# Attention weights turned by DMA: six of eight transposes leave TensorE, and tokens are dealt to the logits' column groups in another way

## The chip, the cores and the metric

The kernel runs on one core of a Trainium2 chip. The metric is the device time of one execution in microseconds, here the median of the runs shown. A profiled execution also gives the span of its trace, which is a little shorter than its device time.

## What is computed

One transformer block with adaptive layernorm over 2048 tokens of width 512, all in bf16. Attention has 32 heads of 16 and looks only at eight earlier tokens, two apart; the second half is a gated feed-forward of width 1792.

```python
def _A_ref(x, wqkv, wo):
    B, S, D = x.shape
    H = 32
    Dh = D // H
    W, dil = (8, 2)
    qkv = (lambda x, *d: x.transpose(*d))((x @ wqkv).reshape(B, S, 3, H, Dh), 2, 0, 3, 1, 4)
    ...
    off = jnp.arange(W) * dil
    idx = pos[:, None] - off[None, :]
    mask = idx >= 0
    ...
    logits = jnp.einsum('bhsd,bhswd->bhsw', q, kg) * scale
    logits = jnp.where(mask[None, None, :, :], logits, -1000000000.0)
    attn = _softmax(logits, axis=-1)
    o = jnp.einsum('bhsw,bhswd->bhsd', attn, vg)
    return (lambda x, *d: x.transpose(*d))(o, 0, 2, 1, 3).reshape(B, S, D) @ wo
...
sa, ca, ga, sb, cb, gb = ...            # six vectors of silu(c) @ w_mod
h = _layernorm(x, axis=-1) * (1 + ca) + sa
x = x + ga * _A_ref(h, A_wqkv, A_wo)
h = _layernorm(x, axis=-1) * (1 + cb) + sb
x = x + gb * _B_ref(h, B_w1, B_w3, B_w2)   # (silu(h @ w1) * (h @ w3)) @ w2
```

## The kernel before

The 2048 tokens are 16 tiles of 128. A tile goes through these steps; the lines are those of the profile.

- Statistics of x on VectorE (L555, L556), a reciprocal square root on GpSimd, and the normalised tile on VectorE (L576). It is transposed on TensorE (L636) or by DMA, and ScalarE or VectorE applies scale and shift (L644, L621). In groups of 2, 2, 4, 4 and 4 tiles, q and k come out transposed (L691), v with tokens on partitions (L711); v is stored to a scratch in DRAM.
- Logits, tile by tile: VectorE multiplies q with eight shifted views of k at once (L742, the first product, 4096 elements a partition), and 16 matmuls with a 0/1 matrix sum over the 16 elements of each head (L752). These use TensorE as four groups of 32 columns, and each group q takes 32 tokens of the tile; the logits stand with 32 heads of group q on partitions 32q to 32q+31, and shift and token in the free dimension. For tile 0, one more matmul first adds the mask of shifts that reach before token 0 (L749).
- Softmax for a pair of tiles at once: four VectorE instructions on PSUM (L764, L769, L794, L796 and the last, L797, which writes the weights to SBUF) with ScalarE's exponential in between (L782). A pair is named here by its first tile: pair 4 is tiles 4 and 5.
- The weights must then stand with token and shift on partitions and heads in the free dimension. For each pair, TensorE transposes four blocks into PSUM (L807) and ScalarE copies them to SBUF (L811).
- Values: per tile four DMA loads of v from the scratch bring shift and token onto partitions ("value loads", sb_vsh and sb_vshx), VectorE multiplies them with the weights (L827), and TensorE sums over the shifts in eight matmuls (L855, "the sums"). ScalarE copies the result (L861), a DMA transpose on SP's queue turns it (sb_ot, "the outputs"), four matmuls apply wo (L867), and VectorE adds the residual (L871).
- Feed-forward in groups of 2, 2, 4, 4, 2 and 2 tiles: layernorm with sums from ScalarE (L590, L601) and GpSimd, transposition, then 14 units of two times four matmuls (L883), silu on ScalarE (L889), gate product on VectorE (L892); then the second matmuls (L921, L909), the output add (L931) and a store.

The six vectors of the modulation are columns computed by matmuls with one column each: L504 for the first layernorm, L531 twice for the two gates, L487 for the second layernorm. wo and w2 are scaled by the gates on VectorE (L946, L952).

Nothing of the order is left to a scheduler at run time: ORDER lists all operations in one sequence, and each engine executes its own in that sequence; nearly all DMAs are issued by SP, in order. An operation waits on semaphores for what it reads and for the last users of the buffer it overwrites; SLOTS says which buffer of a pool each value gets (eight PSUM banks, three for v, three for softmax, and so on). So an instruction that waits holds up all that stand behind it on its engine, and a DMA that waits holds up SP's queue.

Of the kernel before, what the change touches and what calls it, by code (L numbers as in the profile page):

```python
# [6 lines left out]
ACT = mybir.ActivationFunctionType  # L7
# [3 lines left out]
P = 128  # L11
S = 2048
D = 512
H = 32
DH = 16
W = 8
# [57 lines left out]
class Program:  # L74
# [41 lines left out]
    def dma(self, out, in_, key, packets, r=(), w=(), part=(), after=(), eng="sp", cost=450, group=None, transpose=False,  # L116
            store=False, again=False, lat=None):
        nc = self.nc

        def fn(e):  # L120
            a = out() if callable(out) else out
            b = in_() if callable(in_) else in_
            with nc.allow_non_contiguous_dma(reason="layout"):
                return e.dma_start(a, b, transpose=True) if transpose else e.dma_start(a, b)  # L124

        n, size = packets
        each = -(-n // 16)
        ns = 600 if transpose else each * (126 if again else packet_ns(size))
        o = self.op(eng, fn, cost, key, r=r, w=w, part=part, after=after, dma=(each, ns, *(lat if lat else (900, 200) if store else (900, 500) if transpose else (1300, 600))))
        if group is not None:  # L130
            group.append(o)
            o.group = group
        return o
# [135 lines left out]
AC_OLD = ()  # L269
LN1 = [[0, 1], [2, 3], [4, 5, 6, 7], [8, 9, 10, 11], [12, 13, 14, 15]]  # L270


def _build(p, A_x, A_wqkv, A_wo, B_w1, B_w3, B_w2, c, w_mod, out):
# [23 lines left out]
    atb = [sb([P, 2, 32, W], bf, f"attn{i}") for i in range(NSM)]  # L297
    alb = [sb([P, 2, 8, H], bf, f"al{i}") for i in range(3)]
# [94 lines left out]
    for y in range(2):  # L393
# [3 lines left out]
                                           pattern=[[-DIL, W], [1, 2], [2, 16]], channel_multiplier=0), 400, k, w=[vbefore])  # L397
# [333 lines left out]
    def logits(Ts):  # L731

        vl = Val("ps_l", psum)
        for i, T in enumerate(Ts):
# [11 lines left out]
            def red(e, i=i, T=T, vp=vp):  # L746
                c0 = vl.at * 512 + i * W * 32
                if T == 0:
                    e.matmul(PALL[0:32, c0:c0 + W * 32], ones[:, 0:32], before[:], start=True, stop=False, tile_position=(0, 0))  # L749
                for ft in range(KT):  # L750
                    for q in range(4):
                        ins = e.matmul(PALL[32 * q:32 * q + 32, c0:c0 + W * 32], E_sb[:, ft, :], bass.AP(vp.at, ft * P + 32 * q, [[W * KT * P, P], [KT * P, W], [1, 2], [2, 16]]),  # L752
                                       start=(ft == 0 and (T > 0 or q > 0)), stop=(ft == KT - 1), tile_position=(0, 32 * q))
# [35 lines left out]
    def softmax(Ts, vl, ve, vx_):  # L789
# [7 lines left out]
        p.op("dve", lambda e: e.tensor_tensor(ve.at[0][:, 0:n], bass.AP(PALL, bank(vl).offset, [[8 * 512, P], [W * 32, n], [1, 32], [32, W]]),  # L797
                                              bass.AP(ve.at[2], 0, [[64, P], [32, n], [1, 32], [0, W]]), ALU.mult),
             74 + 267 * n, k, r=[vr, vx_], w=[va], hold=[ve, vl], lead=o, lock=False)
        vt, val = Val("ps_at", psum), Val("al", alpool)  # L800

        def turn(e):
            b = bank(vt).bitcast(bf)
            for i in range(n):
                at = b[:, i * 256:(i + 1) * 256].rearrange("p (q y h) -> p q y h", q=4, y=2)
                for y in range(2):
                    ins = e.transpose(at[:, :, y, :], bass.AP(ve.at[0], i * W * 32 + y * 16 * W, [[2 * W * 32, P], [1, P]]), ident[:])  # L807
# [3 lines left out]
        p.op("act", lambda e: e.activation(val.at[:, 0:n].rearrange("p n g h -> p (n g h)"), bank(vt).bitcast(bf)[:, 0:2 * n * P], ACT.Copy),  # L811
# [264 lines left out]
```

## Time and profile before

| | before |
|---|---|
| median of the runs shown | 243.6 us |
| fastest run shown | 243.37 us |
| profiled execution, its own time | 242.82 us |
| span of its trace | 241.1 us |
| granted TensorE clock | 1.0 |
| TensorE (PE) busy | 230.4 us, 1781 matmuls |
| VectorE (DVE) busy | 179.6 us |
| ScalarE (ACT) busy | 138.7 us |
| GpSimd (POOL) busy | 30.9 us |
| moved by DMA | 38.85 MB, 46317 packets |

In the profile a row of a group names line, engine and operation, tile written and tiles read, shapes and count, then the busy time and the mean duration of one, then the idle time ahead of them and what ended it. Matmuls overlap in the pipeline, so the duration of one (219 ns for a 128x128 transpose) is longer than what one adds to the engine's time; the chain and the timeline show the latter, as the time that a run of so many took. "SPq" is the issue of a DMA, whose data land later.

### The profile page before, as it was taken

Reading aid. Unit: us, or ns where it says so; the run is one execution under the profiler, and the core shown is the slowest. Engines: PE = TensorE matmul, PEld = TensorE weight load, DVE = VectorE, ACT = ScalarE, POOL = GpSimd, SP = SyncE. Lnnn points to the kernel's source line nnn. Section 1 sums busy time; section 2 is a strip of 40 time slices with the busy share of each in tenths; the row PEclk is TensorE's granted clock in tenths of the full one; section 3 lists DMA queues with packets and bytes.
Section 4 is the critical chain, followed back from the end, with each engine's and each line's share of the span. In section 5 each row is a group of like instructions: output and inputs, shape, how many; then the busy total and the mean of one; then the engine's idle time right before and its main releaser. Section 6 shows DMA issues by size and latency. Waiting matters only on the chain.

```text
span 241.1 us, 4538 instructions
## 1 busy us (share of the span) xinstructions
PE 230.4 (96%) x1781; PEld 136.8 (57%) x1806; DVE 179.6 (75%) x279; ACT 138.7 (58%) x267; POOL 30.9 (13%) x66
## 2 busy tenths in 40 slices
PE   7988999979999999999799999999999999999995
PEld 4856454544587685564345444444565584485874
DVE  5697999979989999898999999764565044423542
ACT  2296497688999744955964578646537253140300
POOL 4332060004001000250005301001001000000000
PEclk9999999999999999999999999999999999999999
DMA  6999999999979996693893882253220300000103
GB/s 222 370 327 327 163 262 234 287 282 343 331 134 253 283 270 115 160 272 99 213 256 119 195 197 46 66 141 98 76 79 0 46 0 0 3 22 0 48 0 109
DMA packets 46317, 38.85 MB, mean 161 GB/s; under 512 B 21704, under 2 KB 37080, under 8 KB 46296
## 3 DMA queue, kind: packets, MB, share of 16 engines
q1 hardware_dynamic: 46288, 38.56, 62.5%
q8 instruction: 14, 0.23, 0.4%
q14 instruction: 7, 0.06, 0.1%
q10 hardware_dynamic: 8, 0.00, 0.0%
HBM read 29.62 MB, written 4.21 MB: 140 GB/s over the span
## 4 chain that ended last, share of the span: by engine, by line
PE 50%; ACT 1%; DMA 1%; issue 1%; DVE 0%; SPq 0%
PE pall L883 30%; PE pall L921 12%; PE pall L867 3%; PE pall L909 3%; DMA sb_h<-sb_xn 1%; ACT sb_h L621 1%; PE pall L855 1%; PE pall L752 1%; PE pall L807 0%; ACT sb_al L811 0%; DVE sb_o L931 0%; SPq L124 0%
## 5 line engine op out<-in xcount | busy, mean ns | idle before, releaser
L883 PE MATMUL pall<-sb_h,sb_w 128*128 128x256 bf16 (+1 forms) x665 | 101.8, 307 | 1.0 <-ACT sb_h L621 0.6
L883 PEld LDWEIGHTS pall<-sb_h,sb_w 128*128 128x128 bf16 x672 | 64.8, 98 | 36.2 <-issue 1.5
L892 DVE TENSOR_TENSOR sb_hh<-sb_sg,pall 128x256 bf16<-128x256 bf16 (+1 forms) x84 | 40.4, 505 | 32.1 <-PE pall L883 32.0
L889 ACT ACTIVATE sb_sg<-pall 128x256 bf16<-128x256 f32 (+1 forms) x84 | 36.2, 455 | 43.4 <-PE pall L883 37.3
L921 PE MATMUL pall<-sb_w,sb_hh 128*128 128x512 bf16 x189 | 43.7, 379 | 0.4
L742 DVE TENSOR_TENSOR sb_pq<-sb_q,sb_kT 128x4096 bf16<-128x4096 bf16 x16 | 36.3, 2282 | 0.0
L921 PEld LDWEIGHTS pall<-sb_w,sb_hh 128*128 128x128 bf16 x196 | 19.1, 98 | 21.0
L691 PE MATMUL pall<-sb_h,sb_wqkv 128*128 128x512 bf16 (+1 forms) x159 | 30.3, 336 | 0.1
L827 DVE TENSOR_TENSOR sb_vsh<-sb_vsh,sb_al 128x4096 bf16<-128x4096 bf16 x12 | 27.3, 2286 | 2.4 <-ACT sb_al L811 2.2
L621 ACT ACTIVATE sb_h<-sb_h,sb_modc 128x512 bf16<-128x512 bf16 (+1 forms) x24 | 16.3, 733 | 13.0 <-DMA sb_h<-sb_xn 13.0
L691 PEld LDWEIGHTS pall<-sb_h,sb_wqkv 128*128 128x128 bf16 x160 | 15.1, 98 | 12.2 <-ACT sb_h L644 0.5
L931 DVE TENSOR_TENSOR sb_o<-pall,sb_x 128x512 bf16<-128x512 f32 (+1 forms) x18 | 10.9, 627 | 11.8 <-PE pall L921 8.7
L586 POOL TENSOR_SCALAR sb_nm<-sb_sx 128x2 f32<-128x2 f32 x8 | 3.7, 465 | 115.9 <-DVE sb_x L871 115.9
L590 ACT ACTIVATE sb_xn<-sb_x,sb_nm 128x512 bf16<-128x512 bf16 x16 | 11.4, 714 | 11.7 <-POOL sb_nm L586 11.7
L867 PE MATMUL pall<-sb_wo,sb_ot 128*128 128x512 bf16 x60 | 15.0, 379 | 1.1 <-DMA sb_ot<-sb_ac 0.5
L711 PE MATMUL pall<-sb_wqkv,sb_h 128*128 128x512 bf16 x58 | 15.0, 379 | 0.3 <-issue 0.2
L644 ACT ACTIVATE sb_h<-pall,sb_modc 128x256 bf16<-128x256 bf16 (+1 forms) x18 | 9.9, 616 | 8.6 <-DVE sb_modc L509 6.7
L601 ACT ACTIVATE sb_xn<-sb_x,sb_nb,sb_rs 128x512 bf16<-128x512 bf16 x16 | 12.6, 806 | 3.7 <-POOL sb_nb L599 3.7
L871 DVE SCALAR_TENSOR_TENSOR sb_x<-pall,sb_x 128x512 bf16<-128x512 f32 x16 | 11.0, 688 | 2.3 <-PE pall L867 2.3
L701 ACT ACTIVATE sb_kT<-pall 128x512 bf16<-128x512 f32 x16 | 9.6, 606 | 4.7 <-PE pall L691 4.7
L555 DVE BATCH_NORM_STATS2 sb_st<-sb_x 128x6 f32<-128x512 bf16 x16 | 10.4, 678 | 1.3 <-DMA sb_x<-in_A_x_dram 1.3
L721 ACT ACTIVATE sb_v<-pall 128x512 bf16<-128x512 f32 x16 | 9.6, 612 | 2.4 <-DMA v_scratch_dram<-sb_v 2.3
(87 smaller groups left out, 208.6 us busy)
## 6 DMA issues: line engine op xcount, KB each, us to landing
sb_vsh<-v_scratch_dram SPq DMA_DIRECT2D x48, 256.0 KB, 4.6
sb_vshx<-v_scratch_dram SPq DMA_DIRECT2D x16, 256.0 KB, 4.3
sb_w<-in_B_w_dram SPq DMA_DIRECT2D x6, 512.0 KB, 5.6
sb_w<-in_B_w_dram SPq DMA_DIRECT2D x6, 384.0 KB, 6.0
v_scratch_dram<-sb_v SPq DMA_DIRECT2D x16, 128.0 KB, 5.9
out_dram<-sb_o SPq DMA_DIRECT2D x14, 128.0 KB, 1.9
sb_wqkv<-in_A_wqkv_dram SPq DMA_DIRECT2D x6, 256.0 KB, 6.0
sb_x<-in_A_x_dram SPq DMA_DIRECT2D x4, 256.0 KB, 6.3
```

The lines of the kernel that those rows point to most:

```text
L590: p.op("act", lambda e, vn=vn, T=T: e.activation(vn.at[:], x_sb[:, T, :], ACT.Square, bias=nm[:, T, :], accum_out=var[:, T, :]), c_act(512 ...
L601: p.op("act", lambda e, vn=vn, T=T: e.activation(vn.at[:], x_sb[:, T, :], ACT.Identity, bias=nb[:, T, :], scale=rs[:, NT + T, :]), c_act(5 ...
L621: return e.activation(vh.at[:, ft, 0:n * P], vh.at[:, ft, 0:n * P], ACT.Identity, bias=modc[:, 8 * which + ft:8 * which + ft + 1], scale=m ...
L691: ins = e.matmul(bank(vp)[:, j * n:(j + 1) * n], wqkv[:, t, col:col + P], vh.at[:, t, 0:n], start=(t == ORDER[0] and j == 0), stop=(t == O ...
L711: ins = e.matmul(bank(vp), vh.at[:, t, tt * P:(tt + 1) * P], wqkv[:, t, 2 * D:3 * D], start=(t == ORDER[0]), stop=(t == ORDER[-1]))
L742: return e.tensor_tensor(vp.at[:], in0, in1, ALU.mult)
L827: return e.tensor_tensor(v_w, v_w, a_w, ALU.mult)
L867: ins = e.matmul(bank(vy), vt.at[:, ft, :], wo[:, ft, :], start=(ft == 0), stop=(ft == KT - 1))
L883: ins = e.matmul(bank(vp)[:, 0:n], wt[:, t, fi * P:(fi + 1) * P], vh.at[:, t, 0:n], start=(t == 0), stop=(t == KT - 1))
L889: p.op("act", lambda e: e.activation(vt.at[:, 0:n], bank(vgp)[:, 0:n], ACT.Silu), c_act(n), k, r=[vgp], w=[vt], table="silu")
L892: p.op("dve", lambda e: e.tensor_tensor(vh_.at[:, 0:n], vt.at[:, 0:n], bank(vup)[:, 0:n], ALU.mult), c_dve(n), k, r=[vt, vup], w=[vh_])
L921: ins = e.matmul(bank(vz), vhh[fi].at[:, tt * P:(tt + 1) * P], w2[:, fi, :], start=(fi == 0), stop=(fi == NF - 1))
```

## The change

Which 32 tokens of a tile a column group of the logits takes is changed: group q took tokens 32q to 32q+31, even ones first, then odd; now it takes 16 tokens of one parity from each half of the tile. With that, the weights of a pair are four plain blocks of 128 columns, and their transposes are what one DMA transpose of a 128x512 tile gives; the tile order on partitions after it is as before. For pairs 0 and 2 (`AT_PE`) TensorE and ScalarE still do it. For pairs 4, 6, 8, 10, 12 and 14 SP issues one DMA transpose of the shape that the outputs use. The mask for tile 0 follows the new dealing and takes two matmuls. The softmax writes the same elements in the same order; the buffers only change their shape.

ORDER and SLOTS are new as a whole: every engine's sequence changes, the early loads on SP and the places of the FFN units included. Groups, blocks, loads and gates are the same.

```diff
@@ dma(): takes hold=() and hands it on to op()
+AT_PE = (0, 2)
@@ _build
-    atb = [sb([P, 2, 32, W], bf, f"attn{i}") for i in range(NSM)]
-    alb = [sb([P, 2, 8, H], bf, f"al{i}") for i in range(3)]
+    atb = [sb([P, 2 * 32 * W], bf, f"attn{i}") for i in range(NSM)]
+    alb = [sb([P, 4, P], bf, f"al{i}") for i in range(3)]
@@ the mask of tile 0
-                                           pattern=[[-DIL, W], [1, 2], [2, 16]], channel_multiplier=0), 400, k, w=[vbefore])
+                                           pattern=[[-DIL, W], [64, 2], [2, 16]], channel_multiplier=0), 400, k, w=[vbefore])
@@ logits(): red
                 if T == 0:
-                    e.matmul(PALL[0:32, c0:c0 + W * 32], ones[:, 0:32], before[:], start=True, stop=False, tile_position=(0, 0))
+                    for q in range(2):
+                        e.matmul(PALL[32 * q:32 * q + 32, c0:c0 + W * 32], ones[:, 0:32], before[:], start=True, stop=False, tile_position=(0, 32 * q))
                 for ft in range(KT):
                     for q in range(4):
-                        ... bass.AP(vp.at, ft * P + 32 * q, [[W * KT * P, P], [KT * P, W], [1, 2], [2, 16]]),
+                        ... bass.AP(vp.at, ft * P + 32 * (q // 2) + q % 2, [[W * KT * P, P], [KT * P, W], [64, 2], [2, 16]]),
@@ softmax()
-        vt, val = Val("ps_at", psum), Val("al", alpool)
+        val = Val("al", alpool)
+        if Ts[0] not in AT_PE:
+            p.dma(lambda: val.at[:], lambda: ve.at[0][:], ("at", Ts[0]), (128, 1024), r=[va], w=[val], hold=[ve], cost=1270, transpose=True)
+            return val
+        vt = Val("ps_at", psum)
 
         def turn(e):
             b = bank(vt).bitcast(bf)
-            for i in range(n):
-                at = b[:, i * 256:(i + 1) * 256].rearrange("p (q y h) -> p q y h", q=4, y=2)
-                for y in range(2):
-                    ins = e.transpose(at[:, :, y, :], bass.AP(ve.at[0], i * W * 32 + y * 16 * W, [[2 * W * 32, P], [1, P]]), ident[:])
+            for g in range(2 * n):
+                ins = e.transpose(b[:, g * P:(g + 1) * P], ve.at[0][:, g * P:(g + 1) * P], ident[:])
             return ins
@@ ORDER and SLOTS: new lists
```

More of the change, by code (lines that the diff above doesn't have):

```diff
@@ L116, in dma @@
     def dma(self, out, in_, key, packets, r=(), w=(), part=(), after=(), eng="sp", cost=450, group=None, transpose=False,
-            store=False, again=False, lat=None):
+            store=False, again=False, lat=None, hold=()):
         nc = self.nc
@@ L128, in dma @@
         ns = 600 if transpose else each * (126 if again else packet_ns(size))
-        o = self.op(eng, fn, cost, key, r=r, w=w, part=part, after=after, dma=(each, ns, *(lat if lat else (900, 200) if store else (900, 500) if transpose else (1300, 600))))
+        o = self.op(eng, fn, cost, key, r=r, w=w, part=part, after=after, hold=hold, dma=(each, ns, *(lat if lat else (900, 200) if store else (900, 500) if transpose else (1300, 600))))
         if group is not None:
@@ L748, in red @@
                 if T == 0:
-                    e.matmul(PALL[0:32, c0:c0 + W * 32], ones[:, 0:32], before[:], start=True, stop=False, tile_position=(0, 0))
+                    for q in range(2):
+                        e.matmul(PALL[32 * q:32 * q + 32, c0:c0 + W * 32], ones[:, 0:32], before[:], start=True, stop=False, tile_position=(0, 32 * q))
                 for ft in range(KT):
                     for q in range(4):
-                        ins = e.matmul(PALL[32 * q:32 * q + 32, c0:c0 + W * 32], E_sb[:, ft, :], bass.AP(vp.at, ft * P + 32 * q, [[W * KT * P, P], [KT * P, W], [1, 2], [2, 16]]),
-                                       start=(ft == 0 and (T > 0 or q > 0)), stop=(ft == KT - 1), tile_position=(0, 32 * q))
+                        ins = e.matmul(PALL[32 * q:32 * q + 32, c0:c0 + W * 32], E_sb[:, ft, :], bass.AP(vp.at, ft * P + 32 * (q // 2) + q % 2, [[W * KT * P, P], [KT * P, W], [64, 2], [2, 16]]),
+                                       start=(ft == 0 and (T > 0 or q > 1)), stop=(ft == KT - 1), tile_position=(0, 32 * q))
                 return ins
@@ L796, in softmax @@
         o = p.op("dve", lambda e: e.reciprocal(ve.at[2][:, 0:n], ve.at[2][:, 0:n]), 20 + 225 * n, k, r=[vs], w=[vr], hold=[ve, vl], lead=o, lock=False)
-        p.op("dve", lambda e: e.tensor_tensor(ve.at[0][:, 0:n], bass.AP(PALL, bank(vl).offset, [[8 * 512, P], [W * 32, n], [1, 32], [32, W]]),
+        p.op("dve", lambda e: e.tensor_tensor(ve.at[0][:].rearrange("p (n t w) -> p n t w", n=n, w=W), bass.AP(PALL, bank(vl).offset, [[8 * 512, P], [W * 32, n], [1, 32], [32, W]]),
                                               bass.AP(ve.at[2], 0, [[64, P], [32, n], [1, 32], [0, W]]), ALU.mult),
              74 + 267 * n, k, r=[vr, vx_], w=[va], hold=[ve, vl], lead=o, lock=False)
-        vt, val = Val("ps_at", psum), Val("al", alpool)
+        val = Val("al", alpool)
[3 more added lines that the diff above has]
+        vt = Val("ps_at", psum)
         def turn(e):
             b = bank(vt).bitcast(bf)
-            for i in range(n):
-                at = b[:, i * 256:(i + 1) * 256].rearrange("p (q y h) -> p q y h", q=4, y=2)
-                for y in range(2):
-                    ins = e.transpose(at[:, :, y, :], bass.AP(ve.at[0], i * W * 32 + y * 16 * W, [[2 * W * 32, P], [1, P]]), ident[:])
+            for g in range(2 * n):
+                ins = e.transpose(b[:, g * P:(g + 1) * P], ve.at[0][:, g * P:(g + 1) * P], ident[:])
             return ins
         p.op("pe", turn, 114 * n, ("at", Ts[0]), r=[va, vident], w=[vt], hold=[ve])
-        p.op("act", lambda e: e.activation(val.at[:, 0:n].rearrange("p n g h -> p (n g h)"), bank(vt).bitcast(bf)[:, 0:2 * n * P], ACT.Copy),
+        p.op("act", lambda e: e.activation(val.at[:].rearrange("p g q -> p (g q)"), bank(vt).bitcast(bf)[:, 0:2 * n * P], ACT.Copy),
              c_act(256 * n), ("at", Ts[0]), r=[vt], w=[val])
```

127 rows, old and new, of tables (ORDER, SLOTS) are left out of this document.

## The prediction

> **What bounds the kernel now.** I read the page's totals and slices first, then the busy time by stretches, the chain that ended last, the engines' timelines, and last the rows of the operations that the change touches.
>
> ```profile
> span 241.1 us, 4538 instructions
> ...
> PE 230.4 (96%) x1781; PEld 136.8 (57%) x1806; DVE 179.6 (75%) x279; ACT 138.7 (58%) x267; POOL 30.9 (13%) x66
> ```
> ```profile
> 80.00:100.00 20.00, 19.37 (x190) 13.21 (x190) 19.37 (x26) 12.60 (x28) 0.22 (x1) 1.00 0.78 199
> 100.00:120.00 20.00, 18.72 (x143) 10.04 (x143) 18.83 (x24) 14.37 (x25) 4.66 (x7) 1.00 0.79 199
> 180.00:200.00 20.00, 19.89 (x125) 12.26 (x126) 7.54 (x17) 8.69 (x20) 1.30 (x4) 1.00 0.09 14
> ```
> The columns after the length are PE, PEld, DVE, ACT, POOL, the granted clock (1.00 throughout), the DMA share and GB/s. The share of 96% hides two regimes. From 20 to 120 us PE and VectorE are both nearly full; from 120 us VectorE empties and PE alone is full. The chain shows where one hands over to the other:
>
> ```profile
> 110.27 0.49 ACT sb_al L811
> ...
> 110.83 2.44 DMA sb_h<-sb_xn
> ...
> 113.29 2.94 ACT sb_h L621 x4
> ...
> 116.50 5.99 PE pall L883 x27
> 122.49 0.22 PE pall L807 x4
> ...
> 232.34 6.13 PE pall L909 x56
> ...
> 238.49 0.42 DVE sb_o L931
> ```
> At 116.50 the first 512-wide FFN group (tiles 4 to 7) starts; from there PE runs 122.0 us to 238.5 with gaps of at most 0.16, and 2.6 us of adding and storing end the span. What releases 116.50 is a layernorm chain that begins at tile 6's residual add on VectorE:
>
> ```profile
> 102.58 0.68 DVE L871 SCALAR_TENSOR_TENSOR sb_x<-pall,sb_x 128x512 bf16<-128x512 f32 x1
> ...
> 110.78 2.29 DVE L827 TENSOR_TENSOR sb_vshx<-sb_vshx,sb_al 128x4096 bf16<-128x4096 bf16 x1 [1.13 <-ACT sb_al L811]
> ```
> So the path is: VectorE's queue to the add's end (103.2), 13.3 us of statistics, transposes and modulation to 116.5, PE to 238.5, the tail. The bracket is what the change aims at: attention weights turned on PE at 103.1 reached VectorE only at 110.8, because ScalarE's copy of them stood behind work that waited.
>
> **Part 1: the six turns.** Four PE transposes per pair cost 0.22 us (122.49 above), six pairs 1.3 us of PE; the ScalarE copies (L811, mean 598 ns) 3.6 us busy; six PSUM slots go. Of the PE time only pairs 10, 12 and 14 lie after 116.5, where PE sets the pace: 3 x 0.22 = -0.7. Pairs 4, 6 and 8 lie where VectorE paces as well and I count nothing for them; if PE set the pace there too it would be another -0.7. ScalarE's copy at 110.27 was followed by a wait of 2.5 us for the DMA, so its going moves nothing there. The 1.13 us on VectorE disappears, but it lies after 103.2 and what followed it on PE waited 0.67; the new order puts one of the two sums concerned (tile 8's, eight matmuls, 0.43) behind the start of the FFN group: +0.4 on PE's stretch.
>
> What is added are six transposes in SP's queue. The same shape is moved for the outputs already:
>
> ```profile
> L124 SPq DMA_TRANSPOSE sb_ot<-sb_ac x16: 1189/1220/2417, 45.7 to 174.6; - x16
> ...
> DMA to landing us min/median/max: 2.3/3.3/6.0
> ```
> 6 x 1.22 = 7.3 us of SP, which has long waits; per pair the weights come 3.3 us (2.3 to 6.0) after the issue. The cover is VectorE's work between a pair's last softmax instruction and its first value product, counted in the new order by the rows' pitches (2.20 for a product, 0.61 for a 512-wide, 0.33 for a 256-wide gate product): 18, 11, 9.3, 6.8, 3.6 and 8.8 us for pairs 4 to 14. Only pair 12 is near its landing, and there VectorE has room; without cover each would cost 3.3 to 6.0. The waits that come with them are SP's: behind pair 8's transpose stand the four of tiles 4 to 7 that end in 116.5, but its weights are ready at 100 and the first of the four not before 103; behind pair 10's a store, three value loads and tile 9's output; behind pair 14's the outputs of tiles 12 and 13. I take 0. The Trainium skill, page "VectorE: DVE Perf Modes", section "Rules for kernel authors", speaks against this change: turn 128x128 on TensorE where PSUM will do, by DMA otherwise; its table has 390 against 1309 ns. The rows agree in direction (0.22 plus 0.60 against 3.3), and by that rule six exposed turns would cost some 15 us (an estimate from the rows); I don't follow it since the cover hides them.
>
> **Part 2: the dealing of tokens.** The matmuls of L752 read with an outer step of 64 instead of 1; the inner run stays 16 elements of step 2, so 16 of them keep their 0.49 us. The mask of tile 0 needs one more matmul of 32 columns: at most its row's 0.27 us, 0.03 at the pitch. PE's two remaining turns write blocks whole: 0.22 as now. Sum 0; if the outer step cost a tenth, +0.8.
>
> **Part 3: the new order, up to 103.2.** VectorE has less ahead of tile 6's add: three gate products and one output add leave, two gate products come: 0.33 + 0.61 = -0.9. The front loses something. The early loads were issued so:
>
> ```profile
> 8.38 1.97 SPq L124 DMA_DIRECT2D sb_x<-in_A_x_dram  x1
> ...
> 12.46 0.59 SPq L124 DMA_DIRECT2D sb_wm_g<-in_w_mod_dram  x1
> ...
> 18.86 0.50 SPq L124 DMA_DIRECT2D sb_wm_s<-in_w_mod_dram  x1
> ```
> ```profile
> 18.10 0.54 PE L531 MATMUL pall<-sb_csT_bf,sb_wm_g 128*128 128x1 bf16 x16 [0.63 <-DMA sb_wm_g<-in_w_mod_dram]
> ...
> 22.71 0.54 PE L531 MATMUL pall<-sb_csT_bf,sb_wm_g 128*128 128x1 bf16 x16 [0.88 <-DMA sb_wm_g<-in_w_mod_dram]
> ...
> 34.25 0.94 PE L487 MATMUL pall<-sb_csT_bf,sb_wm_s 128*128 128x1 bf16 x32
> ```
> Now the last x load goes ahead of the first gate weights, and PE wants all of the second modulation's weights (L487) some 10 us earlier. The two gate loads landed at about 18.0 and 22.6 with 1.25 MB between them, so 0.5 MB takes 1.8 us: the gate weights come at 19.8 and 21.7, the two halves of the modulation's at 23.5 and 25.4. PE's own work brings it there at 18.3, 20.9 and 24.3: waits of 1.5, 0.8 and 1.1, 3.4 us against 1.5 now, so PE is 1.9 us late. Behind it on PE stand the projections of tiles 4 to 11 and the first logits; behind the gate columns on VectorE stands the first product, which slips from 24.0 to 24.3. PE's delay is then absorbed, since it waits 0.85 and 0.46 us for ScalarE at 49 to 51 now. Three of four parts of wo are also issued later (about 37 instead of 10 to 17); with 6.0 us to landing they come at 44.5 and its scaling on VectorE is reached at 44: 0.5. Together +0.5 on the path, between -0.9 (VectorE's wait for the last x load goes, nothing comes) and +1.9 (PE's whole delay stays).
>
> **Part 4: the new order after 116.5.** The same 512-wide groups with residual adds of tiles 10 and 11 at the same place and those of 8 and 9 eleven us of VectorE work later, still ahead of their use. PE's second group starts three us of PE work later than it did, which gives its layernorm room. I add 0.4 for small waits at the output projections of tiles 8 to 11, whose transposes now share the queue with value loads; 0 to 2.
>
> **The sum.** 241.1 - 0.7 + 0.4 - 0.9 + 0.5 + 0.4 = 240.8 span. The profiled execution took 242.82, 1.7 above its span: 242.5. The median shown is 243.6, 0.8 above that execution: 243.3 by it, 242.5 without it. I say 243.0, which is no measurable change.
>
> **The rivals.**
> - *SP's backlog ahead of pair 12 (slower).* Ahead of that transpose in SP's queue stand twelve value loads and three output transposes, the first held until tile 8's sum is done on PE (about 131.5). At 0.63 and 1.25 us they end at 143 to 144, before the weights are ready at 145.8; landing at 149.1 and two products of 2.2 lead to 153.5, and PE reaches the sums at 155.4. Room: 1.9 us. But six such loads took 7.66 us at 78.2, 1.28 each: then SP comes at 151, the weights land at 155, the sums are ready at 160 and PE waits 4.6. Time 243.0 + 4.6 = 247.6. For it: the room is small, and SP was held 8.1 us on three loads at 125.4. Against it: the DMA share falls to 0.4 there. It decides once SP is more than 1.9 us late. The skill's rule above works this way.
> - *Weights late at the front (slower).* The 1.9 us stay whole and the parts of wo take the 10.0 us that was their worst, 48.5 against 44: up to +4 instead of +0.5; half of that is typical: 244.8. For it: the DMA share is full up to 36 us. Against: VectorE, not PE, paces there.
> - *The waits go (faster).* From 44 to 116.5 PE waits 0.16, 0.85, 0.46, 0.18, 0.51, 0.67 and 0.55, 3.4 in all, for ScalarE, a DMA and VectorE. With ScalarE relieved and slots free, 3 of these could vanish: 240.0. Against: ScalarE is relieved only from pair 4 on, after the two largest.
>
> **How the numbers follow.** The forecast has 0.50, the front 0.20, the backlog 0.15, the waits gone 0.15. The forecast's own range is 241.5 to 244.5. For 8 in 10 I reach to 240.2, next to the centre of the faster case, and 247.2, short of the backlog's. Two per cent, 4.9 us, is about what a measurement of this kernel can tell from no change: faster means under 238.7, which needs the waits gone and part 1's second 0.7 too (0.04); slower means over 248.5, the backlog and the front together or a backlog that meets pair 14 as well (0.11); 0.85 stays.
>
> **What would show it.** Right: two turns at the attention line on PE instead of eight, each DMA turn landing 2.3 to 6.0 us after issue, no VectorE wait on it above 1 us before 130; PE's waits at the gate and modulation weights summing to 2.5 to 4; the 512-wide group starting at 115 to 117, and PE full behind it. Wrong: a PE wait of over 2 us at tile 12's and 13's sums near 155, a VectorE wait for wo near 44, 16 logit matmuls longer than 0.49, or a group start under 114 or over 118.

## The result and the profile after

The changed kernel took 247.37 us against 243.42 in the first comparison (ratio 1.0164, 95% interval 1.0129 to 1.02) and 247.95 against 242.62 in the second (1.0231, 1.0199 to 1.0263). The forecast was 243.0, no measurable change, and the range ended at 247.2: the kernel became slower and left the range. In the first comparison one execution of each kernel was far longer (343.89 us at a granted clock of 0.659, and 303.22 us); the medians include them, the ratio does not. All lines below are of an execution of 247.98 us with a span of 246.2. Line numbers in the changed kernel are one to four higher (L586 is now L587, L883 is L887).

The page's totals (first two lines) and, from the busy time by stretches, two stretches that had been full; columns as before:

```profile
span 246.2 us, 4486 instructions
...
PE 230.7 (94%) x1760; PEld 135.1 (55%) x1783; DVE 178.6 (73%) x279; ACT 135.6 (55%) x261; POOL 30.7 (12%) x66
```
```profile
140.00:160.00 20.00, 18.19 (x122) 8.37 (x124) 17.19 (x27) 10.30 (x19) 2.62 (x8) 1.00 0.83 162
160.00:180.00 20.00, 17.57 (x90) 7.42 (x91) 10.27 (x13) 11.68 (x21) 4.83 (x4) 1.00 0.36 86
```
PE is busy as long as before (230.7 against 230.4 us), the clock is 1.00, and PE has lost its full stretch. In the kernel before, the same two stretches read:

```profile
140.00:160.00 20.00, 19.89 (x110) 9.08 (x110) 17.19 (x23) 14.30 (x24) 1.30 (x4) 1.00 0.44 96
160.00:180.00 20.00, 19.90 (x122) 10.56 (x123) 10.29 (x18) 10.67 (x22) 1.31 (x4) 1.00 0.39 106
```
The PE timeline shows where the stretch begins and what interrupts it; the bracket is the wait ahead of the row:

```profile
117.07 1.24 PE L887 MATMUL pall<-sb_h,sb_w 128*128 128x512 bf16 x5 [0.16 <-issue]
...
143.03 0.81 PE L871 MATMUL pall<-sb_wo,sb_ot 128*128 128x512 bf16 x3 [1.76 <-ACT sb_xn L591]
...
173.34 3.63 PE L887 MATMUL pall<-sb_h,sb_w 128*128 128x512 bf16 x15 [1.65 <-ACT sb_sg L893]
...
178.26 0.61 PE L859 MATMUL pall<-sb_vshx,sb_ind 128*32 128x512 bf16 x8 [0.57 <-ACT sb_sg L893]
...
184.38 4.09 PE L887 MATMUL pall<-sb_h,sb_w 128*128 128x256 bf16 x31 [0.22 <-ACT sb_h L622]
```
The 512-wide group starts 0.57 us later than before (117.07 against 116.50). From there to its last matmul PE took 126.6 us (to 243.7) instead of 122.0: +4.6, of which 4.2 are these four waits. The later start and this stretch, less 0.1 at the tail, are the 5.1 us between the spans.

The wait at 143.03 is put down to ScalarE, but the sequence makes that matmul wait for tile 10's output transpose, which SP issued at 136.31, 6.7 us earlier. The waits at 173 and 178 go back to GpSimd. Rows of the GpSimd, VectorE and ScalarE timelines:

```profile
169.06 2.19 POOL L587 TENSOR_SCALAR sb_nm<-sb_sx 128x2 f32<-128x2 f32 x1 [18.23 <-DVE sb_x L875]
...
172.89 1.74 POOL L597 TENSOR_SCALAR sb_rs<-sb_var 128x2 f32<-128x2 f32 x1 [1.63 <-ACT sb_xn L591]
```
```profile
168.89 2.29 DVE L831 TENSOR_TENSOR sb_vshx<-sb_vshx,sb_al 128x4096 bf16<-128x4096 bf16 x1
```
```profile
171.29 0.72 ACT L591 ACTIVATE sb_xn<-sb_x,sb_nm 128x512 bf16<-128x512 bf16 x1 [4.52 <-POOL sb_nm L587]
```
GpSimd scales two numbers per partition in 2.19 us. It starts just behind a value product of VectorE and ends with it. In the kernel before, the same step for the same tiles had no product beside it:

```profile
162.52 0.22 POOL L586 TENSOR_SCALAR sb_nm<-sb_sx 128x2 f32<-128x2 f32 x1 [15.26 <-DVE sb_x L871]
```
An earlier group of tiles had met a value product (127.69 to 129.98) in the kernel before too:

```profile
127.86 2.19 POOL L586 TENSOR_SCALAR sb_nm<-sb_sx 128x2 f32<-128x2 f32 x1 [19.14 <-DVE sb_x L871]
```
There PE lost nothing: its gaps stay at or below 0.16 us, and behind ScalarE's wait it had logits and sums to do (131.28 to 133.2). As far as these two places show, the meeting costs time where PE next needs what ScalarE holds back. In the changed kernel ScalarE, in order, stands 4.52 us for it; behind its squares stand SiLU copies whose PSUM banks PE wants. The Trainium skill, page "SBUF — State Buffer", section "SBUF: two separate sides", has this: VectorE, in an instruction with two SBUF inputs, and GpSimd lock one pair of ports, and the loser waits out the whole instruction. The trace agrees (2.19 under 2.29).

The weights themselves were not late in this execution. All transposes of them, the waits on them and their landing:

```profile
L124 SPq DMA_TRANSPOSE sb_al<-sb_attn x6: 1204/1272/1310, 73.6 to 160.1; - x6
...
  DMA sb_al<-sb_attn: 0.2, 1
...
DMA to landing us min/median/max: 3.4/4.5/6.6
```

### The profile page after: what moved, and what is told of

The parts are those of the page before. It is cut to its first block, busy times and chain, and to the rows that moved or that the text cites. A ratio compares the mean times of both kernels' runs of the same rounds, so it can differ in the third digit from the quotient of the medians.

```text
span 342.2 us, 4486 instructions
## 1 busy us (share of the span) xinstructions
PE 334.6 (98%) x1760; PEld 164.9 (48%) x1783; DVE 181.0 (53%) x279; ACT 137.2 (40%) x261; POOL 28.5 (8%) x66
## 4 chain that ended last, share of the span: by engine, by line
PE 97%; issue 1%; ACT 0%; DVE 0%; ACTq 0%
PE pall L887 43%; PE pall L925 18%; PE pall L692 12%; PE pall L712 6%; PE pall L871 6%; PE pall L754 3%; PE pall L859 3%; PE pall L913 3%; PE pall L637 1%; PE pall L519 1%; ACT L466 0%; PE pall L488 0%; PE pall L532 0%; PE pall L505 0%; PE pall L811 0%
## 5 line engine op out<-in xcount | busy, mean ns | idle before, releaser
L887 PE MATMUL pall<-sb_h,sb_w 128*128 128x256 bf16 (+1 forms) x666 | 149.8, 402 | 0.9 <-issue 0.5
L887 PEld LDWEIGHTS pall<-sb_h,sb_w 128*128 128x128 bf16 x672 | 79.9, 120 | 72.5 <-issue 48.7
L925 PE MATMUL pall<-sb_w,sb_hh 128*128 128x512 bf16 x189 | 64.2, 512 | 1.0 <-issue 0.4
L692 PE MATMUL pall<-sb_h,sb_wqkv 128*128 128x512 bf16 (+1 forms) x156 | 43.6, 442 | 0.5 <-issue 0.2
L925 PEld LDWEIGHTS pall<-sb_w,sb_hh 128*128 128x128 bf16 x196 | 23.2, 119 | 37.3 <-issue 36.4
L712 PE MATMUL pall<-sb_wqkv,sb_h 128*128 128x512 bf16 x62 | 23.2, 514 | 0.2
L871 PE MATMUL pall<-sb_wo,sb_ot 128*128 128x512 bf16 x60 | 22.2, 510 | 0.7 <-issue 0.4
L587 POOL TENSOR_SCALAR sb_nm<-sb_sx 128x2 f32<-128x2 f32 x8 | 5.7, 711 | 194.9 <-DVE sb_x L875 194.9
L865 ACT ACTIVATE sb_ac<-pall 128x512 bf16<-128x512 f32 x16 | 9.5, 596 | 16.5 <-PE pall L859 16.5
L701 ACT ACTIVATE sb_q<-pall 128x512 bf16<-128x512 f32 x16 | 9.6, 600 | 13.9 <-PE pall L692 13.9
L871 PEld LDWEIGHTS pall<-sb_wo,sb_ot 128*128 128x128 bf16 x64 | 7.8, 123 | 11.5 <-issue 10.8
```

The costliest lines, as they stand in the source:

```text
L692: ins = e.matmul(bank(vp)[:, j * n:(j + 1) * n], wqkv[:, t, col:col + P], vh.at[:, t, 0:n], start=(t == ORDER[0] and j == 0), stop=(t == O ...
L712: ins = e.matmul(bank(vp), vh.at[:, t, tt * P:(tt + 1) * P], wqkv[:, t, 2 * D:3 * D], start=(t == ORDER[0]), stop=(t == ORDER[-1]))
L871: ins = e.matmul(bank(vy), vt.at[:, ft, :], wo[:, ft, :], start=(ft == 0), stop=(ft == KT - 1))
L887: ins = e.matmul(bank(vp)[:, 0:n], wt[:, t, fi * P:(fi + 1) * P], vh.at[:, t, 0:n], start=(t == 0), stop=(t == KT - 1))
L925: ins = e.matmul(bank(vz), vhh[fi].at[:, tt * P:(tt + 1) * P], w2[:, fi, :], start=(fi == 0), stop=(fi == NF - 1))
```

## The experiments

The theory after the first comparison of traces: the loss is the sum of the waits just shown, made by the new order. The main rival: the DMA turns themselves cost, by their landing, by holding the SP queue, or by what they do to other transfers. Ratios are against the kernel before, measured beside each on the same chip; its medians were 242.6 to 243.3 us. A span is that of one execution.

| run | median us | ratio, 95% interval | span |
|---|---|---|---|
| after_look (the change) | 247.95 | 1.0231 [1.0199, 1.0263] | 246.2 |
| deal_only | 242.92 | 1.0013 [0.9995, 1.0031] | 241.1 |
| turns_old_order | 249.6 | 1.0312 [1.0259, 1.0365] | 247.9 |
| new_order_pe | 254.94 | 1.0492 [1.0436, 1.0548] | 254.1 |
| old_turns_468 | 245.27 | 1.0085 [1.0051, 1.012] | 243.6 |
| old_h_first | 248.97 | 1.0231 [1.0185, 1.0277] | 247.1 |
| dup_turns | 248.66 | 1.0249 [1.0183, 1.0314] | 246.1 |
| dup_late | 248.26 | 1.0202 [1.0156, 1.0248] | 245.1 |
| hold_only | 244.24 | 1.0061 [1.003, 1.0091] | 242.1 |
| plain_old | 248.81 | 1.0247 [1.0228, 1.0267] | 246.5 |
| plain_new | 247.5 | 1.0185 [1.0152, 1.0218] | 246.0 |
| tiny_new | 247.77 | 1.0183 [1.0142, 1.0223] | 246.5 |
| ot_first | 248.8 | 1.0236 [1.0203, 1.0268] | 245.9 |
| zo_first | 247.58 | 1.0209 [1.0174, 1.0244] | 245.3 |
| av_after_ln | 247.14 | 1.0174 [1.0136, 1.0212] | 244.7 |
| av_after_ln_ot | 246.29 | 1.0155 [1.0093, 1.0217] | 244.0 |

**The parts of the change, one at a time.** The change as it is:

> The changed kernel once more, for a profile at the full clock. All theories: 247 us, 4 above the kernel before. If the backlog ahead of pair 12's transpose is the cause, PE waits 3 us or more at the sums of tiles 12 and 13 near 155 us and is full up to there; if the front is, the start of the first 512-wide FFN group lies at 119 to 120 instead of 116.5 and no wait of over 1 us follows it.

The dealing alone, in the old order:

```diff
-AT_PE = (0, 2)
+AT_PE = (0, 2, 4, 6, 8, 10, 12, 14)      # and before's ORDER and SLOTS
```


> Before's order and PE turns for all pairs, with only the tokens dealt in the new way (outer step 64 in the logit matmuls, plain blocks in the turns). If the dealing costs nothing, as forecast: 243.4 us. If the strided reads cost the 4 us: 247 us, with 16 logit matmuls taking 0.7 us instead of 0.49.

It costs nothing that can be measured in the time. The logit matmul (L754) went from 270 to 282 ns, the median of 256, and a run of 32 of them from 1.05 to 1.13 us.

The six DMA turns in the old order, at the places of the PE turns:

```diff
+ORDER, SLOTS: before's, each PE turn replaced by the SP turn, ScalarE's copies left out
```


> Before's order and buffers, with the dealing and the six DMA turns put where the PE turns stood; ScalarE's copies are gone. If the DMA turns themselves cost the time (late weights, SP's queue): 246 to 248 us. If the new order does: 241.5 to 243.5 us, about 1 us under before for the PE time saved.

And the new order with all turns on PE, where the DMA turns stood (those of pairs 6 and 8 a few operations later):

> The changed kernel's order with all eight pairs turned on PE and copied by ScalarE, at the places where SP had issued the DMA turns (pairs 6 and 8 a few operations later, where a PSUM bank is free). If the order loses the time by itself, at the front: 247 to 249 us. If the DMA turns do, through SP's queue: 243 to 245 us.

So in the old order six DMA turns cost 6.7 us (249.6 against 242.92). Not all of that is waiting. In its trace PE waits 0.80 and 2.58 us at 157 to 160 us, and behind that the granted clock, the third figure from the end, is lower:

```profile
160.00:180.00 20.00, 19.27 (x87) 7.99 (x90) 8.77 (x11) 10.44 (x21) 1.31 (x4) 0.85 0.33 92
```
It was 0.50 from 160 to 165 us; 15 feed-forward matmuls took 6.1 us there and 3.63 in the row at 173.34 above, so about 2.5 us of the 6.7 are the clock. Its mean was 0.986 to 0.993 in all four executions of this kernel. Why it fell is not shown: in dup_turns below, it stayed at 1.00 behind a wait of 3.20 us.

In the new order PE turns at those places cost more still: one turn stalls PE 2.7 us for weights that aren't ready, and the clock is 0.50 for some 3 us behind it. That kernel also has PE's wait of 1.7 us for the SiLU copies, without any DMA turn.

**Why the turns cost in the old order.** SP's rows there:

```profile
140.68 1.27 SPq L124 DMA_TRANSPOSE sb_h<-sb_xn  x1
148.38 1.19 SPq L124 DMA_TRANSPOSE sb_al<-sb_attn  x1
...
151.57 4.78 SPq L124 DMA_TRANSPOSE sb_h<-sb_xn  x3
```
From 141.95 to 148.38 the queue stands for pair 12's weights, with three feed-forward transposes behind that had begun at 144.55 before. Two runs, one with these transposes ahead, one with only the turns of pairs 4, 6 and 8 (the others on PE). In the lists of the SP queue, tr16 is a feed-forward transpose of tiles 8 to 11, at12 the turn of pair 12, vl12 a value load and ot8 the output transpose of that tile or pair:

```diff
 SP queue:  tr16, at12, vl12, at14, tr16, tr16, tr16
+           tr16, vl12, tr16, tr16, at12, tr16, at14     # old_h_first
```


> The kernel with the six DMA turns at the places of the PE turns in the old order (249.6 us), with one thing changed on the SP queue: the turn of pair 12 is issued behind two more of the feed-forward transposes of tiles 8 to 11 (group 16), and that of pair 14 behind the last of them. Theory 1 (in the old order the turn of pair 12 waits at the head of the SP queue from 141.95 to 148.38 us for its weights, with three feed-forward transposes behind it that had gone out from 144.55 in the kernel before; ScalarE waited 7.1 us for these and PE 2.6 us twice): the transposes go out from about 144.5 again, PE's two waits for the scaled normalised tiles fall from 3.9 us to under 1, and the time falls by 2 to 6 us, to 243.5 to 247.5. Theory 2 (the DMA turn is too long in itself, wherever it stands in the queue: 4.5 us to landing in place of 0.22 us on PE and a copy): PE waits instead at the head sums of tiles 12 and 13, and the time stays at 249 to 250 or grows.

```diff
+AT_PE = (0, 2, 10, 12, 14)               # old_turns_468, before's ORDER
```


> The kernel before with the new dealing of tokens, in the old order, and only pairs 4, 6 and 8 turned by DMA; pairs 0, 2, 10, 12 and 14 on PE. Theory 1 (the cost of the DMA turns in the old order is the SP queue held for pair 12, nothing else): without the turns of pairs 10 to 14 nothing is held, and the time is that of the new dealing alone, 242.9, less up to 0.9 us for three PE turns of 0.22 us and ScalarE copies that are gone: 242.0 to 243.0. Theory 2 (a DMA turn costs by its landing time, 4.5 us, and by what it adds to the SP queue, at every pair): half of the 6.7 us that six turns cost, about 246.

Theory 1 failed in both. With the queue cleared PE's waits for the scaled tiles fell from 3.9 to 1.1 us, but only 0.6 us of time came back: two of the transposes still went out only from 148.53, pair 12's turn not before 153.77, and behind 117 us PE now waited 4.0 us for value products, 2.4 of them at the sums of tiles 12 and 13, as theory 2 had it. The three early pairs cost 2.3 us, though nothing waited for their weights; VectorE waited 1.7 us for value loads. So I separated what a turn does to the queue from what its readers wait for: the turns of deal_only stay on PE, and SP makes an unread copy of each.

```diff
+spares.append(p.dma(spare[j % 2][:], lambda: ve.at[0][:], ("sp_at", Ts[0]), ..., transpose=True))   # dup_turns
```


> The kernel with the new dealing alone (242.9 us), where all eight pairs are turned by PE and copied by ScalarE, and besides six DMA turns of pairs 4 to 14, issued on SP at the places that they had in the kernel with six DMA turns in the old order (249.6 us), into a spare buffer that nothing reads. Theory A (in the old order the turns cost by what they do to the SP queue and the transfers behind them: value loads and feed-forward transposes issued and landed later; the lateness of the weights themselves costs little): most of the 6.7 us shows without any reader, time 246 to 250. Theory B (they cost by their own landing time of 4.5 us ahead of the value products): nothing waits for the spare copies, and the time is 242.9 to 244.

```diff
 dup_turns' list, each spare turn behind 4 to 6 other SP transfers           # dup_late
```


> The kernel with eight PE turns and six DMA turns into a spare buffer (248.7 us), with the six issued later on SP: those of pairs 4 to 10 behind four more of the queue's other transfers each, those of pairs 12 and 14 behind the three feed-forward transposes of group 16, a value load and an attention transpose. The same transfers, but SP no longer stands for softmax weights with other transfers behind it. Theory H (the held queue: SP waits for the weights of a pair while transfers that are ready stand behind): the time falls to 243 to 244.5. Theory T (the traffic: the transfers of the turns themselves, and 1.2 us of SP for each, make value loads and layout transposes late): 246.5 to 249.

```diff
-    ... spare[j % 2][:], lambda: ve.at[0][:], ... transpose=True
+    ... spare[j % 2][0:16, 0, :], lambda: ve.at[0][0:16, 0:P], ...            # hold_only
```


> The kernel with eight PE turns and six DMA turns into a spare buffer (248.7 us), with a plain copy of 4 KB in place of each of the six transposes, at the same places of the SP queue, waiting for the same weights. Theory H (the held queue): the time stays at 246 to 248.7. Theory T (the traffic): 242.9 to 244.

Unread turns cost 5.7 us (248.66 against 242.92): theory A there, and the readers are out of it. The hold alone costs 1.3. Both traces have the same wait of PE, for feed-forward tiles that were transposed late: 3.20 us at 161 in dup_turns, 1.47 at 157 in hold_only. Of dup_turns' four executions the two at a clock of 1.0 took 247.73 and 247.81 us, so 4.8 of the 5.7 stand without the clock. Without the hold the turns cost 5.3 (4.6 by the ratios); of that up to 2.2 is my placement, since two spare turns went ahead of tile 12's output transpose, for which PE waited 2.2. The larger part in the old order is thus neither lateness of the weights nor the hold but the transfers' effect on the others, with the 1.2 us of SP that each takes to issue. Is it the transposition?

```diff
-    ... (128, 1024), r=[va], w=[val], hold=[ve], cost=1270, transpose=True)
+    ... (128, 1024), r=[va], w=[val], hold=[ve])                             # plain_old, plain_new
```


> The kernel with six DMA turns at the places of the PE turns in the old order (249.6 us), with plain copies of the same 128 KB in place of the six DMA transposes (leaves out the turning, so the value products work on weights that are not turned). The SP queue still stands for the weights of pair 12 with three feed-forward transposes behind it. Theory A (the time that the transposes hold the DMA engines is what pairs 4 to 8 cost, 2.3 us, and part of what pairs 10 to 14 cost): the time falls to 245.5 to 247.5; what stays over 242.9 is the held queue. Theory C (the held queue alone makes up the 6.7 us, whatever is issued when it is free again): 249 to 250.

> The changed kernel, in which the six DMA transposes of the attention weights are plain copies of the same 128 KB to the same buffer (leaves out the turning, so the value products work on weights that are not turned); places in the queue, waits and order are the same. Theory A (the DMA transposes cost by the time that they hold the DMA engines: the queue's packets fill 87.6% of 16 engines from 60 to 160 us, against 74.2% with the turns on PE, some 2 us of all engines for each turn, and other transfers land later): the share falls to 76 to 80%, the attention transpose of tile 10 lands in under 5 us, the wait of 1.76 us at 143 us goes, and the time falls from 248.0 to 245.5 to 246.8. Theory B (the order of VectorE, ScalarE and GpSimd sets the time from 110 us on): PE's waits of 1.65 and 0.57 us at 171 to 179 stay and the time stays within 0.6 us of 248.0.

For the most part it is not: plain copies of 128 KB took 0.8 and 0.45 us off (1.6 and 1.1 by the ratios, whose intervals overlap), although SP issues one in 0.5 us instead of 1.2. The busy share of the DMA engines did not fall as expected either (83.8 to 83.4% in the old order, 87.6 to 85.3% in the new), so that my 2 us of all engines for each transposition does not hold. How the cost of six 128 KB transfers divides between the engines' time, SP's time and the order of landing in the queue stays open.

**Why the new order costs.** The same question in the changed kernel, with 4 KB copies in place of the turns:

```diff
-    p.dma(lambda: val.at[:], lambda: ve.at[0][:], ... (128, 1024), ... transpose=True)
+    p.dma(lambda: val.at[0:16, 0, :], lambda: ve.at[0][0:16, 0:P], ... (16, 256), ...)   # tiny_new
```


> The changed kernel, in its own order, with a plain copy of 4 KB in place of each of the six DMA transposes of the weights (leaves out the turning: the value products work on weights of other pairs or zeros, and the buffer that no PE turn fills is zeroed once on GpSimd at the start); queue, waits and order are the same. In the old order such copies cost 1.2 us where transposes cost 5.9. Theory T (the traffic of the turns makes other transfers late in the new order too): the share of the DMA engines falls from 87.6% to 75 to 80%, the time falls by 3 to 4.5 us, to 243.5 to 245. Theory O (the new order itself is longer, and the turns' traffic costs little in it): PE's waits of 1.65 and 0.57 us at 171 to 179 stay and the time stays at 246.8 to 248.

Theory O: the time hardly moves. The share of the DMA engines fell only to 84.5%, not to 75 to 80%, so most of its rise belongs to the new order as well. The PE timeline has the same wait at the same place:

```profile
173.35 3.63 PE L887 MATMUL pall<-sb_h,sb_w 128*128 128x512 bf16 x16 [1.65 <-ACT sb_sg L893]
```
With almost no traffic of the turns, but with SP's waits for the weights, which these copies keep, the new order is still 4.4 us longer than the kernel before (1.0183), so it is there that the waits must be undone. First the loads ahead of tile 10's output transpose:

```diff
 SP queue:  ot8, vl15, vl12, ot10, vl13, vl13, ot11
+           ot8, ot10, vl13, vl13, ot11, vl15, vl12       # ot_first
```


> The changed kernel, with two value loads (one of pair 12's second half of the loads, one of tile 15's) issued on the SP queue behind the attention transposes of tiles 10 and 11 instead of ahead of tile 10's. Nothing else moves. Theory 1 (the loss behind 117 us is a sum of separate waits, the first being tile 10's transpose, issued at 136.31 and needed by PE at 141.3, which landed 6.7 us after its issue behind two 256 KB loads): the transpose lands in 3 to 5 us, PE's wait of 1.76 us ahead of the output projection of tile 10 falls under 0.5 us, and the time falls by 1.2 to 1.8 us, to 246.2 to 246.8. Theory 2 (the new order is paced by VectorE up to 141 us, and what PE doesn't lose there it loses at the next value of VectorE's or ScalarE's): the wait at 143 us shrinks but the time stays within 0.5 us of 248.0.

The wait at 143 went, as expected, but the time did not: 0.55 us came back as a wait for a value product at 158.88, for which VectorE, now earlier, had waited 1.00 us for pair 12's turned weights, and the wait of 1.65 us at the SiLU copies now ended at 172.91, only 0.43 earlier. Theory 2 here: behind this wait stood the next one. Then the product that lies over GpSimd's step (rs13 is the residual add of tile 13, av15 the value product of tile 15, zo5 a feed-forward output add):

```diff
 VectorE:  rs13, rs12, av15, zo5, zo6, av14
+          rs13, rs12, zo5, zo6, av15, av14               # zo_first
```


> The changed kernel, with one VectorE instruction moved: the 2.29 us value product of tile 15, which came right behind the additions of tiles 12 and 13, is put behind the two gated outputs (1.28 us) that came next. Theory 1 (the 2.29 us product held GpSimd's scaling of the layernorm sums, 2.19 us in place of 0.22, ScalarE's squares stood behind that, the SiLU copies behind the squares, and PE waited 1.65 and 0.57 us for PSUM banks): the GpSimd instruction at 169 us takes under 0.5 us, ScalarE's wait of 4.52 us for it falls to 2.5 to 3, PE's waits of 1.65 and 0.57 us fall to a sum under 0.8, and the time falls by 1.2 to 2.0 us, to 246.0 to 246.8. Theory 2 (the length of GpSimd's small instructions has nothing to do with the product beside it, or ScalarE is held by something else): the instruction keeps 2 us or the PE wait comes back at the second GpSimd step, and the time stays within 0.5 us of 248.0.

The first step shrank to 0.22 us and ScalarE's wait for it to 2.54 us, both as expected. But the products now lay over the next two steps:

```profile
168.49 0.22 POOL L587 TENSOR_SCALAR sb_nm<-sb_sx 128x2 f32<-128x2 f32 x1 [18.36 <-DVE sb_x L875]
170.34 1.51 POOL L597 TENSOR_SCALAR sb_rs<-sb_var 128x2 f32<-128x2 f32 x1 [1.63 <-ACT sb_xn L591]
171.94 2.63 POOL L598 TENSOR_TENSOR sb_rs<-sb_rs,sb_cst 128x2 f32<-128x2 f32 x1
```
and PE's wait of 1.65 us moved to the sums, at 176.22. So the products were made to wait for GpSimd's last step, then also with the loads moved (lines one higher again):

```diff
+          rs13, rs12, zo5, zo6, av14, av15               # av_after_ln
+        p.ops[580].deps[p.ops[953]] = True               # av14 waits for GpSimd's last step
```


> The changed kernel, with the two 2.29 us value products of tiles 14 and 15 put behind the two gated outputs that follow the additions of tiles 12 and 13, tile 14's first, and with the first of them made to wait for GpSimd's last step of the layernorm of tiles 12 and 13, so that none of its four small steps can lie beside a product. Theory 1 (these steps, 2.19, 1.74, 0.71 and 0.20 us beside the products, hold ScalarE's squares and normalised tiles, behind which the SiLU copies stand; when only the first was freed, the second and third took 1.51 and 2.63 and PE's wait of 1.65 us moved to the head sums): the four steps take under 1.4 us together, GpSimd is done by about 171.8 in place of 175.7, PE's waits of 1.65 and 0.57 us between 171 and 179 fall to a sum under 0.8, and the span falls by 1.5 to 2.5 us, to 243.7 to 244.7 (time 245.4 to 246.5). Theory 2 (VectorE's own order is what holds PE there, and moving its products later only moves the wait): PE waits 1 to 2 us for the value products at the head sums of tiles 14 and 15, and the span stays within 0.7 us of 246.2.

```profile
169.25 0.22 POOL L588 TENSOR_SCALAR sb_nm<-sb_sx 128x2 f32<-128x2 f32 x1 [18.34 <-DVE sb_x L876]
171.10 0.19 POOL L598 TENSOR_SCALAR sb_rs<-sb_var 128x2 f32<-128x2 f32 x1 [1.64 <-ACT sb_xn L592]
171.38 0.70 POOL L599 TENSOR_TENSOR sb_rs<-sb_rs,sb_cst 128x2 f32<-128x2 f32 x1
172.16 0.19 POOL L601 TENSOR_TENSOR sb_nb<-sb_nm,sb_rs 128x2 f32<-128x2 f32 x1
```


> The same as the kernel with the products behind the layernorm steps of tiles 12 and 13, and besides the two value loads issued behind the attention transposes of tiles 10 and 11. Theory 1 (both waits are real, but each hid behind the other: with the loads moved alone, the 1.39 us gained at 141 us were given back by 0.55 us at the head sums of tile 12 and by the wait at 171, which ended only 0.43 us earlier): the sum of both, 2.2 to 3.5 us, shows now: span 242.7 to 244.0, time 244.4 to 245.7. Theory 2 (VectorE's order paces the stretch from 141 to 180 as a whole): within 0.5 us of the kernel with the products moved alone.

GpSimd's four steps took 1.3 us together, and the span fell by 1.5, with both edits by 2.2 (to 244.0): the collision and the late transpose make these waits. The times fell by 0.8 and 1.7 us (to 246.29), less surely: the intervals overlap with that of the change, though the three executions of the last kernel at a clock of 1.0 (245.26 to 246.86 us) lie below all four of the change (247.71 to 248.57). Its span is still 2.9 above that of the kernel before. What is left behind 117 us in it are PE's waits of 0.93 and 1.21 us for value products. The first is the DMA turn itself: VectorE waited 1.38 us for pair 12's weights, whose turn was issued at 149.23 and whose product began at 154.28. The second follows 2.08 us in which VectorE was made to wait for GpSimd by this very edit. No version beat the kernel before, and deal_only equals it.

## Why the prediction was wrong

- *Part 1, the turns.* The cover taken at 0 was right for what it counted: in the new order VectorE waited 0.2 us for the weights, although they landed in 3.4 to 6.6 us, median 4.5, instead of 2.3 to 6.0, median 3.3. For pair 12, where the prediction saw room on VectorE, that was partly luck: with tile 10's transpose on time VectorE did wait for these weights, 1.00 us in ot_first and 1.38 in av_after_ln_ot, and PE 0.55 and 0.93 behind it. The prediction counted only the readers of the weights. What six more transfers do to those beside them had no term; in the old order that is some 4 of 6.7 us (5.7 for unread turns less 1.3 for the hold, a lower clock included), in the new one it is 0.2 us by the medians and 1.2 by the ratios (tiny_new against the change), so this omission is not the main part of the miss.
- *Part 2, the dealing.* Right for the time (deal_only). The logit matmuls did lengthen, by 0.08 us for a run of 32 and so by some 0.6 us of PE in all (an estimate for 256); that is nearer to the prediction's 0.8 for a longer step than to its 0, and most of it lies ahead of the group's start.
- *Part 3, up to the group's start.* The waits for gate and modulation weights came where they were forecast, but sum to 1.7 us, not 3.4, and less than the 2.5 named as right. VectorE's wait for wo was 0.90 instead of 0.5; the prediction named such a wait as a sign of being wrong, though its own sum held one. Tile 6's add ended at 103.7 where the terms -0.9 and +0.5 put it at 102.8, and the group started at 117.07 instead of 116.1, just outside the 115 to 117 named as right. About 1 us of the miss.
- *Part 4, after 116.5.* This step failed. It had "0.4 for small waits at the output projections of tiles 8 to 11", with a range of 0 to 2, and PE full behind the group's start. One wait was of that kind, at tile 10, and measured 1.76. The others are of a kind that I had not priced: layernorm steps on GpSimd under value products, ScalarE's queue behind them, SiLU copies behind that: 1.65 and 0.57. The kernel before shows such a step (2.19 us at 127.86, above), but off PE's path; the prediction has no term for GpSimd's steps, nor for where a new order of VectorE puts its products over them. Stretch after the start: +4.6 measured against +0.1 summed.
- *The rivals.* SP's backlog did not appear: SP stood free for pair 12's weights, which were ready only at 150.8 instead of 145.8, and PE did not wait at the sums (158.88). That its price of 247.6 us lies next to the measured time is chance. In old_h_first its mechanism is there: the turn went out at 153.77 behind other transfers, and PE waited 2.4 us at these sums. The front rival was half there in kind, small in size. The waits did not go.
- Against the sum of 240.8 the span is 5.4 longer: about 1.0 in Part 3, 4.5 in Part 4, -0.1 in the tail.

## What to carry to other kernels

Where a kernel's engine is full behind one point, price a new order by the waits of that engine behind the point, and for every small instruction of GpSimd there ask which long product of VectorE will lie over it and what stands in order behind the engine that waits for it. Move a load, and look where the next wait stands: here one wait of 1.76 us undone alone gave no time (248.8 us against 247.95), undone together with those behind GpSimd 1.7 us, and one more, for a DMA turn, came to light behind them. A transfer that nothing waits for isn't free in a queue that is three quarters full: measure it as an unread copy.

## What the runs showed of the hardware

Six unread 128 KB transfers between SBUF buffers cost 5.7 us of 243 in the old order, and as plain copies, read, little less than as transposes (248.81 against 249.6), while copies of 4 KB at the same places cost 1.3. GpSimd's instructions on 128x2 elements took 0.19 to 0.22 us alone, one of them 0.70, and 1.51 to 2.63 where they began early under VectorE's 2.29 us products of two SBUF operands, until about the end of the product. Behind PE's waits of 0.80 and 2.58 us the granted clock was 0.50 for some 5 us in one kernel, and it stayed at 1.00 behind a wait of 3.20 us in another.
